# One head pair of a pooled attention taken from fp32 transposes on TensorE to fp16 parts and DMA transposes

## The chip, the core and the metric

The kernel runs on one core of a Trainium2 chip. The metric is the device time in microseconds of one execution. A core has five engines with their own in-order queues: TensorE (PE; its weight loads are listed as PEld), VectorE (DVE), ScalarE (ACT), GpSimd (POOL) and SyncE (SP), which here only issues DMAs to 16 DMA engines.

## The reference

Attention with pooled queries, then a feed-forward block (FFN), in fp32:

```python
q_pool = q.reshape(B, H, S // 2, 2, D).mean(axis=3)      # B=4, H=8, S=1152, D=64
scores = matmul(q_pool, k^T) / sqrt(D)
attn = softmax(scores)                                   # 576 x 1152 for each of 32 heads
x = matmul(attn, v), heads side by side                  # 2304 x 512
h = x @ w_in                                             # 512 -> 2048
g = relu(h) ** 2
out = g @ w_out                                          # 2048 -> 512
```

## The kernel before

**Pairs and chunks.** Two heads form a pair, so there are 16 pairs, four for each batch. A pair has nine chunks of 128 query rows, 144 chunks in all, numbered from 0. For a chunk the kernel computes on TensorE the scores against 1152 keys into PSUM (S, lines 739 to 760), on VectorE their maximum (MX, line 771), on ScalarE the exponential (EX, line 795), which leaves P as 128x1152 fp32 in SBUF. P must then be transposed, so that keys lie on partitions, before it is multiplied by V (PV). The transposed chunks lie in one tile, PT. A pair's chunks form two groups, r0 (four chunks) and r1 (five), and each group has one PV.

**Two ways to transpose.** For pairs listed in the option FV, P stays fp32: nine fp32 transposes on TensorE into PSUM (TP, line 836), copied to PT three at a time by ScalarE or VectorE (TC, lines 846 and 848), and a PV of 36 fp32 matmuls (line 947). For all other pairs P is split into two fp16 parts: the high part (HI, ScalarE, line 799), the rest (LO, GpSimd or VectorE, line 807); both are transposed by one DMA on SyncE's queue (TR, line 810), and the PV has three products, 108 fp16 matmuls (line 955). V is split in the same manner for these pairs (VA line 343 or 345, VD line 374), and a small addition (MB, lines 778 and 781) scales P. In the kernel before FV holds pairs 0 to 3, which are batch 0.

PT is shared by both ways, and they lay it out differently. Chunks of the other layout may be written only when every PV of the layout before has been computed; chunks of the same layout wait only for the PV whose columns they overwrite (function ringof). With the option PART the groups of pairs 2 and 3 come in the order r0 of pair 2, r0 of pair 3, r1 of pair 2, r1 of pair 3.

**FFN.** When a batch's pairs are done, blocks of 256 tokens go through the FFN: per block eight first products H (line 1119, 24 matmuls), each followed by a ReLU (HA, lines 1129 and 1131), a square in fp16 (G1, line 1134), a square in fp32 (G2, lines 1139 and 1142) and their difference (G3, line 1146), and eight second products O (line 1168, 12 matmuls). There are nine blocks. Their weights are split into fp16 parts at the start (lines 1222 to 1347). FFN work of earlier batches is mixed between the chunks of later ones; the last three blocks follow the last chunk.

**What sets the order.** The class Plan holds every step with its engine or engines, its cost and what it needs. It lists the steps by simulated start times; offsets by kind of step ('off', and 'off0' for the first part) and slacks by engine ('slPE' and so on) decide between ready steps, and which engine takes a step that has a choice. The program is then written out in that order, so every engine's queue is fixed. Seven buffers of 128x2304 fp16 hold P and its parts, two raw tiles hold loads, two PSUM tiles hold scores, and two PSUM banks hold everything else until the last chunk.

Of the kernel before, what the change touches and what calls it, by code (L numbers as in the profile page):

```python
# [16 lines left out]
AX = mybir.AxisListType  # L17
PSUM = bass.MemoryType.PSUM

CFG = {'SPLIT': 0, 'TURN': [], 'TURNB': [], 'WDP': ((1, 0), (1, 1), (1, 2), (1, 3)), 'WSP': 0.4394, 'WOF': 23.2581, 'MSP': 10.7319, 'pen': 4650.4498, 'bl': 16.0216, 'slPE': 66.7964, 'slACT': 353.0356, 'slDVE': 0.0, 'slPOOL': 569.0059, 'slSP': 247.8544, 'off': {'ED': 1246.3547, 'EX': 5849.5041, 'G1': -389.0426, 'G2': -104.1829, 'G3': 554.5948, 'GE': 1873.7106, 'GF': -32.4945, 'GM': -760.1485, 'GR': 210.7973, 'GS': 94.4545, 'H': 960.6071, 'HA': -234.5462, 'HI': -641.2151, 'KA': -143.9903, 'KC': -8.1783, 'KD': 872.723, 'KT': -553.181, 'KX': -147.2817, 'LF': 208.5276, 'LK': -464.9703, 'LO': 615.8798, 'LQ': 735.5594, 'LV': 186.7785, 'MB': 263.0646, 'MX': 219.6772, 'O': 959.2234, 'OD': -6.8812, 'PV': 582.1743, 'QA': -1778.9621, 'QC': -65.0614, 'QD': -30.2052, 'QK': 1295.5337, 'QQ': -170.0803, 'QS': 1636.5642, 'QT': 389.6557, 'QV': 96.5433, 'QX': 1378.7913, 'QY': 11.4121, 'RB': -182.8597, 'RT': -62.6818, 'RU': -185.4151, 'RV': 888.0764, 'S': 448.8179, 'ST': -370.0893, 'TC': -3741.4466, 'TP': 227.7703, 'TR': 3470.1614, 'U0': -286.6317, 'U1': -121.9166, 'U2': 428.2909, 'U4': -13.234, 'U5': -34.8662, 'UA': -25.2061, 'UB': 489.5818, 'UD': -136.1539, 'UG': -386.0049, 'UL': -18.9466, 'UM': 385.026, 'US1': 86.5628, 'US2': 126.1804, 'US3': 177.5466, 'VA': -449.2776, 'VD': -50.9897, 'W0': 92.9318, 'W1': -160.9693, 'W2': 2408.4173, 'W4': 41.9909, 'W5': -49.6702, 'WA': -177.1177, 'WD': 4887.2789, 'WG': 51.2485, 'WL': -84.1217, 'WM': -759.71, 'WS1': -97.3652, 'WS2': -484.1136, 'WS3': -24.1358, 'XA': 3.5042, 'XD': 344.6772, 'XM': 149.4019, 'XN': -648.326, 'XO': -302.7277, 'XQ': 72.8927, 'XR': 25.0451, 'XT': 74.8128, 'XU': -26.4071, 'XW': -53.316, 'aG1': 975.376, 'aG2': -8.3412, 'aG3': 1812.5384, 'aH': 945.5101, 'aHA': 95.0276, 'aO': 944.1552, 'aOD': 737.0717, 'aRB': -107.2593, 'aRT': -33.339, 'aRU': -29.5278, 'aRV': 101.1642, 'aST': -112.5231, 'aXA': -332.137, 'aXD': -1.658, 'aXM': -134.621, 'aXN': 37.6008, 'aXO': 26.3067, 'aXQ': 42.9163, 'aXR': 1688.4275, 'aXT': -68.0245, 'aXU': 17.1682, 'aXW': 186.1889, 'zG1': 91.0859, 'zG2': 58.4733, 'zG3': 647.1768, 'zH': -71.0289, 'zHA': -90.6818, 'zO': -226.9787, 'zOD': -96.8945, 'zRB': 31.1111, 'zRT': 315.2862, 'zRU': 90.4617, 'zRV': -0.3031, 'zST': -3.2166, 'zXA': -0.3901, 'zXD': -290.7, 'zXM': 77.2111, 'zXN': 89.9134, 'zXO': -46.2986, 'zXQ': 96.7, 'zXR': 171.8139, 'zXT': -141.9837, 'zXU': 189.9734, 'zXW': -22.7318}, 'off0': {'ED': -0.1938, 'EX': 44.7507, 'G1': 37.0992, 'G2': 58.5453, 'G3': -179.5235, 'GE': 422.2703, 'GF': -3.4782, 'GM': 45.9462, 'GR': -673.3064, 'GS': 105.2042, 'H': 24.4643, 'HA': -223.3679, 'HI': -0.3824, 'KA': -287.1981, 'KC': 265.8239, 'KD': 60.1455, 'KT': 47.8024, 'KX': -28.954, 'LF': 2579.7627, 'LK': 334.2631, 'LO': -615.0613, 'LQ': -324.4973, 'LV': -104.7173, 'MB': 34.3544, 'MX': -0.4589, 'O': 221.9113, 'OD': -64.4508, 'PV': -177.1018, 'QA': 354.2099, 'QC': 78.2737, 'QD': -44.0538, 'QK': -43.1499, 'QQ': 328.969, 'QS': 153.2762, 'QT': -555.006, 'QV': -66.5589, 'QX': -187.5264, 'QY': -268.1213, 'RB': -32.6021, 'RU': -78.4363, 'RV': 5.802, 'S': 2.838, 'ST': -2.5942, 'TC': 45.0906, 'TP': -907.5806, 'U0': 36.9458, 'U1': -33.4125, 'U2': 285.286, 'U4': 104.4439, 'U5': 15.7265, 'UA': 719.2255, 'UB': 70.692, 'UD': 144.5044, 'UG': 106.0304, 'UL': 11.0132, 'UM': 73.0092, 'US1': 161.6416, 'US2': -3.3033, 'US3': 328.9473, 'VA': 5.0083, 'VD': 0.3732, 'W0': 160.5816, 'W1': -301.2958, 'W2': -204.9077, 'W4': -25.4103, 'W5': -205.3827, 'WA': -279.8196, 'WD': -6.6893, 'WG': -22.2842, 'WL': -342.4531, 'WM': 192.4837, 'WS1': -321.4596, 'WS2': -444.2766, 'WS3': -35.6721, 'XA': 154.1639, 'XD': -16.0094, 'XM': 58.2004, 'XN': -133.1141, 'XO': 39.0783, 'XQ': -62.6032, 'XR': -9.301, 'XT': 225.4302, 'XU': -208.803, 'XW': -31.9494, 'aG1': -6.3492, 'aG2': -53.3067, 'aG3': -123.269, 'aH': -2.0139, 'aO': 367.1081, 'aOD': -23.0563, 'aRB': -38.5418, 'aRT': -62.2213, 'aRU': -52.5422, 'aRV': -10.1497, 'aST': -203.7505, 'aXD': -771.7661, 'aXM': -273.1333, 'aXN': -91.8521, 'aXO': 34.8573, 'aXQ': -0.2413, 'aXR': -502.6026, 'aXU': 52.3162, 'aXW': -13.8618, 'zG1': 8.5148, 'zG2': -475.2825, 'zG3': 47.993, 'zH': 315.6821, 'zHA': -17.051, 'zO': 53.7112, 'zOD': -299.6009, 'zRB': 117.4021, 'zRT': -17.2734, 'zRU': -54.008, 'zRV': 84.2467, 'zST': 346.2005, 'zXA': 239.278, 'zXD': -8.2809, 'zXM': -91.6437, 'zXN': -36.4568, 'zXO': 47.406, 'zXQ': -130.928, 'zXR': 322.459, 'zXT': -469.0206, 'zXU': -229.1112, 'zXW': -385.6444}, 'FV': (0, 1, 2, 3), 'PART': 1, 'QXD': (1, 2, 3, 4), 'MSC': (0, 1, 2, 3, 4, 5, 6, 7, 8, 9, 10, 11, 12, 13, 14, 15), 'FS': (0,), 'NSG': (12, 13, 14, 15)}  # L20
# [4 lines left out]

# [1433 lines left out]
```

## Time and profile before

| | us |
|---|---|
| three runs | 793.77, 796.21 (median), 802.07 |
| profiled execution | 796.25 |
| its span | 794.4 |
| PE busy | 743.8 (94%) |
| ACT busy | 589.7 (74%) |
| DVE busy | 571.4 (72%) |
| POOL busy | 350.1 (44%) |
| mean granted TensorE clock | 0.973 of 2.4 GHz |

The span runs from the first to the last instruction; 1.9 us of the profiled execution lie outside it. Busy shares are of the whole span; the kernel has a first part (weights, batch 0), a long middle part (chunks and FFN mixed) and a last part (FFN alone), so shares must be read by stretch.

### The profile page before, as it was taken

What the parts mean: (1) busy time and instruction counts of PE and PEld (TensorE: products, weight loads), DVE (VectorE), ACT (ScalarE), POOL (GpSimd) and SP (SyncE); (2) the same over time, 40 slices, a digit from 0 to 9 for tenths busy, and PEclk for the clock granted to TensorE, in tenths of its full rate; (3) what the DMA queues carried; (4) which work ended last, traced back from release to release, by engine and by line L of the source; (5) the groups of instructions that cost most, each with busy time, mean ns of one, the idle gap of its engine ahead of it and who ended that gap; (6) DMA issues with size and microseconds to landing.
All of it is one profiled execution on the core that took longest, in us unless ns stands there. A gap on an engine that the chain in (4) does not pass through costs nothing.

```text
span 794.4 us, 15338 instructions
## 1 busy us (share of the span) xinstructions
PE 743.8 (94%) x5998; PEld 491.7 (62%) x5998; DVE 571.4 (72%) x920; ACT 589.7 (74%) x874; POOL 350.1 (44%) x240
## 2 busy tenths in 40 slices
...
DMA  8686573417889999999999999999999991000011
GB/s 325 225 233 187 167 204 106 120 31 142 168 172 199 194 225 218 219 206 215 186 212 199 217 208 207 202 228 195 209 217 191 173 183 25 1 2 13 14 27 28
DMA packets 324840, 128.96 MB, mean 162 GB/s; under 512 B 307104, under 2 KB 307872, under 8 KB 324768
## 3 DMA queue, kind: packets, MB, share of 16 engines
...
## 4 chain that ended last, share of the span: by engine, by line
PE 78%; DVE 7%; ACT 5%; DMA 5%; issue 3%; SPq 1%; POOL 0%; DVEq 0%; ACTq 0%; POOLq 0%
PE ba L1168 17%; PE ba L1119 17%; PE s L760 12%; PE ba L955 10%; PE bt L1168 7%; PE bt L1119 6%; DVE s L771 3%; PE ba L836 3%; DMA region<-in_moe_w_in_dram 2%; PE ba L947 2%; ACT buf L795 2%; PE s L755 2%; DMA w<-in_moe_w_out_dram 2%; DVE PT L848 1%; ACT PT L846 1%
## 5 line engine op out<-in xcount | busy, mean ns | idle before, releaser
L771 DVE TENSOR_SCALAR_CACHE_REDUCE s<-s,esc 128x1152 f32<-128x1152 f32 x135 | 190.9, 1420 | 32.2 <-PE s L760 21.9
L1119 PEld LDWEIGHTS <-w 128*128 128x128 f16 x1728 | 169.4, 99 | 33.1 <-issue 7.0
L795 ACT ACTIVATE buf<-s,ca 128x1152 f32<-128x1152 f32 x144 | 174.4, 1212 | 14.2 <-DVE s L771 7.7
L807 POOL TENSOR_TENSOR buf<-buf,buf 128x1152 f16<-128x1152 f32 x53 | 130.9, 2472 | 54.1 <-ACT buf L799 44.2
L760 PE MATMUL s<-kT,qT 128*128 128x512 f16 x720 | 137.6, 330 | 9.3 <-ACT buf L795 9.0
L1168 PE MATMUL ba<-w,region 128*128 128x512 f16 x624 | 142.2, 379 | 1.3 <-ACT region L1129 0.7
L1168 PEld LDWEIGHTS <-region 128*128 128x128 f16 x864 | 82.8, 98 | 96.3 <-issue 2.5
L1119 PE MATMUL ba<-region,w 128*128 128x256 f16 x1104 | 128.7, 275 | 1.3 <-DVE x L1046 1.2
L799 ACT ACTIVATE buf<-buf 128x1152 f16<-128x1152 f32 x107 | 124.5, 1163 | 5.9 <-DMA PT<-buf 1.7
L760 PEld LDWEIGHTS <-qT 128*128 128x128 f16 x720 | 63.6, 100 | 66.9 <-issue 18.1
L807 DVE TENSOR_TENSOR buf<-buf,buf 128x1152 f16<-128x1152 f32 x55 | 77.1, 1404 | 14.4 <-ACT buf L799 14.1
L955 PE MATMUL ba<-PT,v 128*64 128x320 f16 (+1 forms) x1296 | 85.4, 290 | 0.0
L955 PEld LDWEIGHTS <-v 128*64 128x64 f16 x1296 | 70.8, 111 | 14.7 <-issue 7.1
L1146 POOL TENSOR_TENSOR region<-region 128x512 f16<-128x512 f32 x35 | 49.2, 1405 | 51.4 <-ACT region L1139 50.0
L1146 DVE TENSOR_TENSOR region<-region 128x512 f16<-128x512 f32 x37 | 29.1, 793 | 58.7 <-ACT region L1139 55.8
L836 PE MATMUL ba<-ident,buf 128*128 128x128 f32 x324 | 54.4, 296 | 14.8 <-ACT buf L795 5.5
L1134 ACT ACTIVATE region<-region 128x512 f16<-128x512 f32 x72 | 45.1, 626 | 20.3 <-PE bt L1168 17.3
L836 PEld LDWEIGHTS ba<-ident,buf 128*128 128x128 f32 x324 | 36.4, 148 | 30.7 <-ACT PT L846 8.7
L1168 PE MATMUL bt<-w,region 128*128 128x512 f16 x240 | 52.6, 379 | 0.0
L1142 POOL TENSOR_TENSOR region<-region 128x512 f32<-128x512 f32 x11 | 14.6, 1329 | 83.6 <-ACT region L1134 83.6
L846 ACT ACTIVATE PT<-ba 128x384 f32<-128x384 f32 x76 | 35.7, 490 | 18.6 <-PE ba L836 17.1
L1119 PE MATMUL bt<-region,w 128*128 128x256 f16 x432 | 48.7, 273 | 0.0
...
## 6 DMA issues: line engine op xcount, KB each, us to landing
...
```

What stands on the lines that cost most here:

```text
L760: nc.tensor.matmul(s[:, x, :w], lhsT=qt[:, l].rearrange("p c m -> p (c m)")[:, 128 * c0 + h : 128 * c0 + h + 255 : 2], rhs=rhs, **st)
L771: nc.vector.tensor_scalar(st3(), st3(), sc, 3e38, op0=ALU.mult, op1=ALU.min, accum_out=a[:, x : x + 1])
L795: nc.scalar.activation(P(), st3(), AF.Exp, bias=a[:, 1:2], scale=s1, accum_out=col)
L799: nc.scalar.activation(hl()[:, 0], P(), AF.Copy)
L807: e.tensor_tensor(out=hl()[:, 1], in0=P(), in1=hl()[:, 0], op=ALU.subtract)
L836: nc.tensor.matmul(t[:, y], lhsT=P()[:, c * 128 : (c + 1) * 128], rhs=ident, is_transpose=True, start=(y == 0), stop=(y == 2), skip_group_ ...
L846: nc.scalar.activation(out, t, AF.Copy)
L955: nc.tensor.matmul(px[h * 64 : (h + 1) * 64, 64 * r * (1 - h) : 64 * r * (1 - h) + N], lhsT=vv[:, h, kc, vl, :], rhs=p2(vi, r, h, 9 * pl + ...
L1119: nc.tensor.matmul(ph[:, f2], lhsT=w16[0][:, SLOT[f // 4], wl, a, f % 4 * 128 : (f % 4 + 1) * 128], rhs=xhl()[:, xl, a], start=(i == 0), s ...
L1134: nc.scalar.activation(gt[u][:, 0], rt[u % 2], AF.Square)
L1146: e.tensor_tensor(out=gt[u][:, 1], in0=rt[u % 2], in1=gt[u][:, 0], op=ALU.subtract)
L1168: nc.tensor.matmul(p[:, :DM], lhsT=g[:, gl, f % 2, tt * 128 : (tt + 1) * 128], rhs=w16[1][:, SLOT[f // 4], wl, f % 4], start=(f == 0 and g ...
```

## The change

FV loses pair 3, and the numbers that set the order are new (252 offsets and ten other numbers; the engines that may take a step are the same):

```diff
-CFG = {... 'WSP': 0.4394, 'WOF': 23.2581, 'MSP': 10.7319, 'pen': 4650.4498, 'bl': 16.0216, 'slPE': 66.7964, ...
+CFG = {... 'WSP': 1.0247, 'WOF': 22.4804, 'MSP': 10.4991, 'pen': 6462.0091, 'bl': 16.654, 'slPE': 128.9911, ...
...
-... 'FV': (0, 1, 2, 3), 'PART': 1, 'QXD': (1, 2, 3, 4), ...
+... 'FV': (0, 1, 2), 'PART': 1, 'QXD': (1, 2, 3, 4), ...
```

So the groups r0 of pair 2, r0 of pair 3, r1 of pair 2, r1 of pair 3 now change PT's layout three times instead of once after them.

SyncE's queue before, from pair 4's query transpose on (kT and qT are transposed keys and queries of a pair, PT<-buf is TR of a chunk): the first TR is pair 4's, behind the key and query transposes of pair 5.

```order
L646 DMA_TRANSPOSE qT_105<-half_100 128x9x128
L652 DMA qT_105<-qT_105 64x1152 x2
L633 DMA_TRANSPOSE kT_103<-buf_93 128x18x128
L455 DMA raw_102<-in_k_dram 128x2x576
L463 DMA raw_101<-in_q_dram 64x1152 x2
L455 DMA raw_101<-in_v_dram 128x2x576
L633 DMA_TRANSPOSE kT_104<-buf_98 128x18x128
L455 DMA raw_102<-in_k_dram 128x2x576
L646 DMA_TRANSPOSE qT_106<-half_100 128x9x128
L810 DMA_TRANSPOSE PT<-buf_95 128x18x128
L810 DMA_TRANSPOSE PT<-buf_93 128x18x128
```

And now: four TR of pair 3's r0 with a weight load and a load of values between them, then pair 4's keys and queries, then the TR of pair 3's r1.

```order
L810 DMA_TRANSPOSE PT<-buf_99 128x18x128
L1222 DMA w_1_91<-in_moe_w_out_dram 128x2x1024
L810 DMA_TRANSPOSE PT<-buf_98 128x18x128
L810 DMA_TRANSPOSE PT<-buf_94 128x18x128
L455 DMA raw_102<-in_v_dram 128x2x576
L810 DMA_TRANSPOSE PT<-buf_95 128x18x128
L646 DMA_TRANSPOSE qT_105<-half_100 128x9x128
L633 DMA_TRANSPOSE kT_103<-buf_97 128x18x128
L455 DMA raw_101<-in_k_dram 128x2x576
L652 DMA qT_105<-qT_105 64x1152 x2
L810 DMA_TRANSPOSE PT<-buf_97 128x18x128
L810 DMA_TRANSPOSE PT<-buf_93 128x18x128
```

Nine TR more stand ahead of pair 4's, and pair 5's keys and queries, which stood ahead of pair 4's first TR, now stand on either side of it.

ScalarE's queue before, in front of pair 4's first exponential, chunk 36 (the last row; sums_87 is the batch's row sums, L846 a copy of transposed P, L343 on w and v a high part of a weight or of V).

```order
L343 ACTIVATE v_0_107<-raw_101,psc 128x18x64
L1343 ACTIVATE w_1_91<-w_1_91,wS_1313 128x2048
L846 ACTIVATE PT<-ba_114 128x3x128
L846 ACTIVATE PT<-ba_115 128x3x128
L846 ACTIVATE PT<-ba_114 128x3x128
L846 ACTIVATE PT<-ba_115 128x3x128
L795 ACTIVATE buf_94,sums_86<-s_113,ca 128x1152
L846 ACTIVATE PT<-ba_115 128x3x128
L795 ACTIVATE buf_96,sums_87<-s_112,ca 128x1152
```

And now, in front of the same exponential (L1129, L1134 and L1139 are FFN steps, L778 is MB).

```order
L778 ACTIVATE ca<-ca,cols 128x1
L1134 ACTIVATE region<-region 128x512
L1139 ACTIVATE region<-region 128x512
L1129 ACTIVATE region<-ba_114 128x512
L1134 ACTIVATE region<-region 128x512
L1139 ACTIVATE region<-region 128x512
L778 ACTIVATE ca<-ca,cols 128x1
L1129 ACTIVATE region<-ba_115 128x512
L343 ACTIVATE half_100<-raw_102,psc 128x9x64
L1134 ACTIVATE region<-region 128x512
L1139 ACTIVATE region<-region 128x512
L795 ACTIVATE buf_94,sums_87<-s_112,ca 128x1152
```

The exponential of chunk 36 stood at place 162 of ScalarE's queue and stands at 184; FFN steps that came behind it come before it.

## Rows read from the trace of the kernel before

**Rows 1.** The page: busy time of each engine; share of the 16 DMA engines by 40 slices.
```profile
PE 743.8 (94%) x5998; PEld 491.7 (62%) x5998; DVE 571.4 (72%) x920; ACT 589.7 (74%) x874; POOL 350.1 (44%) x240
...
DMA  8686573417889999999999999999999991000011
```

**Rows 2.** Stretches: length; busy PE, PEld, DVE, ACT, POOL; clock; DMA share; GB/s.
```profile
160.00:200.00 40.00, 33.00 (x242) 20.55 (x243) 31.23 (x66) 38.03 (x53) 23.82 (x12) 0.98 0.47 93
200.00:229.00 29.00, 29.00 (x245) 21.27 (x244) 22.47 (x34) 23.75 (x36) 21.71 (x14) 0.91 0.82 150
229.00:300.00 71.00, 70.00 (x604) 46.58 (x602) 62.36 (x89) 61.06 (x92) 45.38 (x31) 1.00 1.11 211
...
600.00:652.00 52.00, 52.00 (x459) 34.11 (x458) 42.54 (x63) 44.08 (x64) 21.98 (x15) 1.00 1.00 179
652.00:794.00 142.00, 137.77 (x1006) 91.87 (x1004) 32.97 (x63) 46.58 (x74) 10.27 (x10) 0.99 0.09 20
```

**Rows 3.** The chain of waits between 229 and 652 us, shares by line.
```profile
by line: PE ba L1168 27.8%; PE ba L1119 23.8%; PE s L760 19.9%; PE ba L955 17.3%; PE s L755 2.3%; issue 1.5%; DMA raw<-in_v_dram 1.1%; DVE s L771 0.9%; ACT buf L795 0.8%; DVE region L1046 0.7%; DVE buf L807 0.6%; PE ba L591 0.5%; POOL half 
```

**Rows 4.** Groups by line (the first of all shapes): count | busy, mean ns | idle before.
```profile
L760 PE MATMUL s<-kT,qT 128*128 128x512 f16 x720 | 137.6, 330 | 9.3 <-ACT buf L795 9.0
L836 PE MATMUL ba<-ident,buf 128*128 128x128 f32 x324 | 54.4, 296 | 14.8 <-ACT buf L795 5.5 <-DVE PT L848 4.6 <-ACT PT L846 3.4
L947 PE MATMUL ba<-PT,v 128*64 128x320 f32 x144 | 20.3, 435 | 0.6 <-DVE PT L848 0.6
L947 PE MATMUL ba<-PT,v 128*64 128x256 f32 x144 | 16.4, 382 | 0.3 <-ACT PT L846 0.3
L955 PE MATMUL ba<-PT,v 128*64 128x320 f16 x648 | 47.7, 306 | 0.0
L955 PE MATMUL ba<-PT,v 128*64 128x256 f16 x648 | 37.7, 273 | 0.0
```

**Rows 5.** The same view: work of ScalarE, and the two forms of LO.
```profile
L846 ACT ACTIVATE PT<-ba 128x384 f32<-128x384 f32 x76 | 35.7, 490 | 18.6 <-PE ba L836 17.1 <-DVE PT L848 0.2
L1134 ACT ACTIVATE region<-region 128x512 f16<-128x512 f32 x72 | 45.1, 626 | 20.3 <-PE bt L1168 17.3 <-DVE region L1131 1.6
L1139 ACT ACTIVATE region<-region 128x512 f32<-128x512 f32 x59 | 37.2, 630 | 1.8
L778 ACT ACTIVATE ca<-ca,cols 128x1 f32<-128x1 f32 x42 | 12.3, 292 | 21.4 <-DVE s L771 20.3 <-DVE xs L363 0.3
L343 ACT ACTIVATE buf<-raw,psc 128x1152 f16<-128x1152 f32 x4 | 5.0, 1242 | 0.0
L799 ACT ACTIVATE buf<-buf 128x1152 f16<-128x1152 f32 x107 | 124.5, 1163 | 5.9 <-DMA PT<-buf 1.7
L807 POOL TENSOR_TENSOR buf<-buf,buf 128x1152 f16<-128x1152 f32 x53 | 130.9, 2472 | 54.1 <-ACT buf L799 44.2 <-issue 7.7 <-POOL esc L368 1.1
L807 DVE TENSOR_TENSOR buf<-buf,buf 128x1152 f16<-128x1152 f32 x55 | 77.1, 1404 | 14.4 <-ACT buf L799 14.1
```

**Rows 6.** The source view of line 810: durations, first and last start; time to landing.
```profile
L810 SPq DMA_TRANSPOSE PT<-buf x108: 2400/2840/5931, 191.1 to 652.0; - x108
...
DMA to landing us min/median/max: 4.5/5.2/8.4
```

**Rows 7.** SyncE's timeline: start, duration, instruction, count.
```profile
258.81 1.40 SPq L463 DMA_DIRECT2D raw<-in_q_dram  x2
260.31 10.09 SPq L810 DMA_TRANSPOSE PT<-buf  x3
...
280.09 4.28 SPq L810 DMA_TRANSPOSE PT<-buf  x1
```

**Rows 8.** ScalarE's timeline: the exponential of chunk 56.
```profile
266.79 1.22 ACT L795 ACTIVATE buf<-s,ca 128x1152 f32<-128x1152 f32 x1
```

**Rows 9.** TensorE's timeline: the first FFN products, in brackets the idle time ahead.
```profile
182.09 2.78 PE L1119 MATMUL ba<-buf,w 128*128 128x256 f16 x24 [0.18 <-DVE psc L601]
199.31 5.28 PE L1119 MATMUL ba<-buf,w 128*128 128x256 f16 x24 [3.68 <-DVE region L1046]
```

2 lines of the change are left out of this document (1 added, 1 removed).

## The prediction

> **What bounds the kernel now.** I read the page first [rows 1]. TensorE is busy 94% of the span, and the DMA slices stand at 9 from about 220 us on, until they drop to 0 and 1 near 655 us. So two resources are nearly full over most of the span, and which one sets the pace has to be read by stretch. The windows [rows 2] show three parts. Up to about 229 us neither is full: between 160 and 200 us TensorE works 33.00 of 40 us and the DMA share is 0.47, while ScalarE works 38.03 of 40. From 229 to 652 us TensorE is full (70.00 of 71, 52.00 of 52) and the DMA share is 1.11 at the front and 1.00 at the back. From 652 us on only FFN is left: TensorE 137.77 of 142 us, DMA 0.09.
>
> The chain of waits over the middle [rows 3] is nearly all TensorE: products of the FFN, of the scores and PV, and 1.1% DMA. Read alone it says that TensorE is the bound. But the source view of the transposes [rows 6] and SyncE's timeline [rows 7] say something else. 108 TR start between 191.1 and 652.0 us, one in 4.3 us, and in the timeline one instruction starts as the one before it ends (258.81 + 1.40 to 260.31), so at that place the queue has no gap. Chunk 56 shows what it means: its exponential starts at 266.79 us and takes 1.22 [rows 8], HI takes 1.16 and LO on GpSimd 2.47 [rows 5], so P could go out at 271.6. Its TR starts at 280.09 [rows 7]: it stands 8.5 us behind the queue. The middle is therefore held from both sides: the queue sets when P arrives, and TensorE fills what is left with FFN work. Saving TensorE time there shortens the run only as far as the stream of TR moves too.
>
> **The change, part by part.**
>
> *TensorE.* Removed are 9 x 9 = 81 fp32 transposes of 54.4 / 324 = 0.168 us, 13.6 us, and two fp32 PV of (20.3 + 16.4) / 8 = 4.6 us each, 9.2 us. Added are two fp16 PV of (47.7 + 37.7) / 24 = 3.6 us, 7.1 us [rows 4]. The sum is -15.7 us; the small products by which pair 3's values get their scale take some of it back, so I use -15. This work lies ahead of pair 4, where TensorE is not full: at the share of 160 to 200 us, 33.00 / 40 = 0.83 [rows 2], some 12 us of it are on a path.
>
> *The DMA queue.* Nine more TR of 2.84 us, 25.6 us [rows 6]. They go out ahead of pair 4's first TR (191.1), among slices of DMA that read 3, 4, 1 and 7 tenths [rows 1], so I cost their bandwidth at nothing. The cover is the 0.53 of the share that is free between 160 and 200 us, 21 us, and more ahead of it; were it gone, 25.6 us would come upon every later TR. Bounds: 0 and +25.6; I take 0, for the rows at the place itself are the nearest.
>
> The Trainium skill, page "VectorE: DVE Perf Modes", sections "The three transpose paths" and "Rules for kernel authors", speaks against the change: it gives 390 ns for a 128x128 bf16 block on TensorE and 1309 ns by DMA, and advises TensorE where PSUM can take the result. By it the 9 x 18 blocks would be an estimated 212 us of the queue. The trace does not agree on the figure: 18 blocks go out in 2.84 us [rows 6], 0.16 us each, no more than an fp32 block on TensorE.
>
> *ScalarE.* 17 copies of transposed P go (-8.3 us at 0.490), nine HI come (+10.5 at 1.163) [rows 5]; the total is nearly unchanged, but its place is not. By the two lists of ScalarE's order, ahead of chunk 56's exponential there are now nine more HI (+10.5), seven more G1 and G2 each (+8.8 at 0.626 and 0.630), five more fp16 splits of V (+6.2 at 1.242), seven more MB (+2.0 at 0.292), and the 17 copies less (-8.3) [rows 5]: +19.2 us. The exponential comes later by what ScalarE cannot fit into its idle time. It worked 38.03 + 23.75 + 61.06 = 122.8 of the 140 us from 160 to 300 us, 0.88; if it fills up to the 0.95 of 160 to 200 us [rows 2], the 107 us up to this exponential give 0.07 x 107 = 7.5 us. Left are 11.7 us, and the 8.5 us in which this chunk's P waited for the queue hide most of that. So the stream of TR from there on is **3 us late**. Bounds: 0 (ScalarE fills up completely) and +11 (it fills up by nothing: 19.2 - 8.5). I take 3, from the row of the same stretch.
>
> *VectorE and GpSimd.* There are ten fewer copies on VectorE. Of the 117 LO, GpSimd now has 76 where it had 53, VectorE 41 where it had 55 [rows 5]. GpSimd gains 23 x 2.47 = 57 us of LO and has 350.1 us of work in all [rows 1]; it stays far from full. VectorE gets 20 us free. For a chunk with no time in the queue a LO on GpSimd is 1.07 us later than one on VectorE; where P waits 8.5 us that is hidden. I cost it at nothing and keep it as a rival.
>
> *Layouts of PT.* Three switches in place of one. At each of the two new ones towards DMA the TR must wait for the PV before. I cost them at nothing in the forecast, because first FFN products exist by 182.09 us [rows 9] and can stand in for pair 3's second wait; the first wait is a rival.
>
> *What comes back later.* From pair 6's products on, TensorE has 15 us less to do than before at the same place of the stream. It can gain them only if TR follow. At 600 to 652 us the share is 1.00 and at 229 to 300 us 1.11 [rows 2], so the later queue has room, but the bound from below is 0 and from above 15 (TensorE's own saving). The rows say that both are full and not which gives way first, so I take half, -7. The part after the last PV, 142 us [rows 2], is the same work in both and stays.
>
> **Sum.** +3 - 7 = -4 us. The profiled execution took 796.25 us (span 794.4), 0.04 above the median of 796.21, so the sum needs no shift: 796.25 - 4 = **792 us**.
>
> **The rivals.**
>
> *A, the forecast:* the queue takes back most of TensorE's gain. 792 us; by its bounds (+11 with nothing back is 807, 0 with all 15 back is 781) and half of each, its own range is 787 to 800. Chance 0.48, of which 0.06 lie below 788.2.
>
> *B, TensorE is the bound all along.* For it: the chain [rows 3] with 1.1% DMA, and 52.00 of 52 us. Against it: the wait of chunk 56's P for its TR [rows 7, 8]. Then the 12 us that are on a path reach the end: 796 - 12 = 784 us. Chance 0.26.
>
> *C, slower: the new switch of layout at pair 3's r0.* Its four TR may not go before pair 2's r0 has its PV, and pair 3's r0 product needs all four: 4 x 2.84 + 5.2 us to landing [rows 6] = 16.6 us. In that time TensorE has no FFN work (the first H stands after it) and pair 2's r1 may not be transposed into PT, since it has the other layout. Two score tiles let it compute the scores of two chunks, 2 x 137.6 / 144 = 1.9 us [rows 4]. It idles some 14 us, and may then run at half clock: 24 matmuls took 5.28 us after 3.68 us of idle time, against 2.78 [rows 9]. It decides once the wait goes beyond the 1.9 us, and if the later part gives nothing back: 796 + 14 = 810 us. Against it: TensorE has 17% idle time there already, part of which may be the same wait. Chance 0.18. Only by such a wait, not by its price for a block, would the advice of the Trainium skill hold.
>
> *D, LO on GpSimd.* Where P does not wait for the queue, 23 LO that come 1.07 us later hold the stream up; a third of them in such places are 8 x 1.07 = 9 us on top of the forecast: 801 us. For it: 1.00 of DMA at the end, where the queue has room and P is late. Against it: VectorE is less loaded, so LO can start sooner. Chance 0.08.
>
> **How the numbers follow.** The likeliest is A, 792 us. About 1% is what a measurement of this kernel can tell from no change: 788.2 and 804.2 us. Faster: B's 0.26 and 0.06 of A, 0.32. Slower: C's 0.18, 0.02 of A, and 0.02 of D, 0.22. The same: 0.46. The range reaches from B's side, some 2 us below its 784, to C's 810: 782 to 810.
>
> **What would show it.** TensorE's busy time falls to about 729 us and the last stretch after the last TR stays at 142 us: then the sum on TensorE is right, and the run's change is the move of the last TR away from 652.0. For A, chunk 56's exponential starts later than 266.79 by about 12 us, its TR by some 3, and the last TR starts 4 us earlier. For B, the exponential and the stream start earlier and DMA shares in the middle rise. For C, an idle stretch of some 14 us on TensorE stands ahead of pair 3's first fp16 product with DMA as the releaser, and slow matmuls after it. For D, the chain of waits shows LO of GpSimd in the middle. The forecast is wrong if the middle's queue packs tighter than 1.11, or if ScalarE fills its idle time so fully that chunk 56 is not late.

## The result, and the profile after

The changed kernel takes 806.9 us (median of four runs, 803.8 to 808.7) against 797.0 before: 1.1% slower, ratio 1.0113 with a 95% interval of 1.0075 to 1.0151. Forecast were 792 us and a range of 782 to 810; the time lies in the range, but the kernel became slower where a gain was forecast; the chance given to slower was 0.22.

The page, as [rows 1]: busy times, and the DMA share by slices of a fortieth of the span.

```profile
PE 736.9 (92%) x5964; PEld 487.3 (61%) x5964; DVE 580.1 (72%) x922; ACT 595.3 (74%) x876; POOL 376.7 (47%) x247
...
DMA  8687548738999999999999999999999992000011
```

TensorE works 6.9 us less, the span (804.9 us) is 10.5 longer, so TensorE idles 17.4 us more. The groups of TensorE, as [rows 4] (the fp16 PV of one group is 54 matmuls; 108 are the two groups of a pair):

```profile
L760 PE MATMUL s<-kT,qT 128*128 128x512 f16 x720 | 141.2, 337 | 13.0 <-ACT buf L795 13.0
...
L836 PE MATMUL ba<-ident,buf 128*128 128x128 f32 x243 | 39.2, 288 | 12.0 <-ACT PT L846 6.8 <-DVE PT L848 3.3 <-ACT buf L795 1.8
...
L947 PE MATMUL ba<-PT,v 128*64 128x320 f32 x108 | 15.2, 435 | 0.0
L947 PE MATMUL ba<-PT,v 128*64 128x256 f32 x108 | 14.0, 420 | 2.1 <-DVE psc L601 1.9 <-ACT PT L846 0.3
...
L955 PE MATMUL ba<-PT,v 128*64 128x320 f16 x702 | 51.1, 300 | 0.8 <-DMA PT<-buf 0.7
L955 PE MATMUL ba<-PT,v 128*64 128x256 f16 x702 | 43.2, 280 | 2.5 <-DVE psc L601 1.6 <-DMA PT<-buf 0.4 <-DVE region L1131 0.4
```

Transposes 54.4 to 39.2, fp32 PV 36.7 to 29.2, fp16 PV 85.4 to 94.3: -13.8 us, close to the -15 of the sum. Some of it goes at once: the scores of line 760 take 141.2 us where they took 137.6, the same matmuls, with a lower granted clock in the stretches from 300 to 400 us below.

The windows show where the rest went (columns as in [rows 2]); first the changed kernel from 120 us on, then three stretches of the kernel before that [rows 2] lack.

```profile
120.00:160.00 40.00, 27.22 (x256) 17.85 (x255) 35.16 (x62) 26.75 (x40) 17.51 (x11) 0.91 0.79 186
160.00:200.00 40.00, 34.62 (x279) 25.46 (x278) 32.17 (x51) 38.57 (x51) 26.92 (x14) 1.00 0.54 96
229.00:300.00 71.00, 70.74 (x570) 46.12 (x569) 61.06 (x87) 61.34 (x91) 43.68 (x28) 1.00 1.08 207
300.00:340.00 40.00, 31.97 (x229) 17.60 (x228) 31.13 (x53) 31.73 (x49) 23.77 (x12) 0.84 1.07 210
340.00:400.00 60.00, 51.49 (x449) 37.34 (x447) 48.09 (x86) 46.65 (x71) 33.82 (x21) 0.82 1.07 198
663.00:805.00 142.00, 137.21 (x1004) 91.69 (x1003) 34.43 (x64) 44.70 (x72) 9.58 (x11) 1.00 0.09 20
```

```profile
120.00:160.00 40.00, 33.43 (x282) 21.46 (x280) 31.51 (x63) 31.66 (x49) 9.90 (x7) 1.00 0.38 106
300.00:340.00 40.00, 40.00 (x306) 22.52 (x306) 29.54 (x47) 29.98 (x44) 20.49 (x15) 1.00 1.11 209
340.00:400.00 60.00, 53.10 (x467) 37.04 (x463) 49.74 (x90) 52.96 (x78) 34.10 (x24) 0.89 1.06 205
```

Two holes: 120 to 160 us (27.2 of 40 us, clock 0.91) and 300 to 400 us (83.5 of 100, clock 0.82 to 0.84; before 93.1). The last stretch is the same 142 us.

The first hole lies among the switches of PT's layout. TensorE's timeline has pair 3's first fp16 product (54 matmuls of line 955) and pair 2's r1 product (line 947); SyncE's has the last transfer ahead of pair 3's r1 and the first of its TR; SyncE's list of waits, 100 to 230 us, says what held TR (total, times, longest).

```profile
149.18 3.14 PE L955 MATMUL ba<-PT,v 128*64 128x256 f16 x54 [1.62 <-DVE psc L601]
...
169.88 5.07 PE L947 MATMUL ba<-PT,v 128*64 128x320 f32 x36
```

```profile
150.42 1.15 SPq L652 DMA_DIRECT2D qT<-qT  x2
175.03 9.14 SPq L810 DMA_TRANSPOSE PT<-buf  x3
```

```profile
SPq L810 <- DVE PT L848: 14.4, 1, 14.4
SPq L810 <- PE ba L947: 9.5, 2, 9.0
```

From 151.6 to 175.0 us SyncE stands with pair 3's r1 TR at the head of its queue: pair 2's r1 may go into PT only after the fp16 product of 149.18, needs its transposes and copies, and gives PT free when its own product ends at 175.0. That is a wait of the queue. TensorE's own waits from 120 to 160 us name exponentials (6.6 us), a scale (1.6) and loads (2.3), and no TR, so it is not shown that the switch makes the hole.

In the second hole TensorE has no FFN left. Its timeline: scores at full rate, the last product of batch 0's FFN, scores that wait for exponentials, the first H of batch 1.

```profile
312.77 1.14 PE L760 MATMUL s<-kT,qT 128*128 128x512 f16 x6
313.74 2.75 PE L1168 MATMUL ba<-w,region 128*128 128x512 f16 x12
...
335.11 2.08 PE L760 MATMUL s<-kT,qT 128*128 128x512 f16 x6 [1.91 <-ACT buf L795]
...
363.34 2.78 PE L1119 MATMUL ba<-region,w 128*128 128x256 f16 x24
...
369.88 2.13 PE L755 MATMUL s<-kT,qT 128*64 128x512 f16 x12 [3.42 <-ACT buf L795]
```

Six score products of line 760 take 2.08 us there and 1.14 us at 312.77; the granted clock is 0.84 from 300 to 340 us and 1.00 before. So there is no FFN product from 316.5 to 363.3 us, 46.9 us. In the kernel before that gap is 23.9 us long; its timeline has the last product of batch 0's FFN and the first H of batch 1 at

```profile
332.76 2.75 PE L1168 MATMUL ba<-w,region 128*128 128x512 f16 x12
...
359.38 2.78 PE L1119 MATMUL ba<-region,w 128*128 128x256 f16 x24
```

The stream of transposes, as [rows 6], and chunk 56, as [rows 7, 8]: its exponential (ScalarE) and its TR (SyncE).

```profile
L810 SPq DMA_TRANSPOSE PT<-buf x117: 2397/2862/6071, 127.7 to 663.3; - x117
```

```profile
280.07 1.20 ACT L795 ACTIVATE buf<-s,ca 128x1152 f32<-128x1152 f32 x1
```

```profile
291.37 4.10 SPq L810 DMA_TRANSPOSE PT<-buf  x1
```

The exponential is 13.3 us late (12 were forecast), its TR 11.3 (3 were forecast), and the last TR 11.3 (4 us early was forecast). Chunk 56 has 15 H and 9 O ahead of its exponential, 8 and 8 in the kernel before, so part of its delay is FFN work done earlier.

Much below is read from ScalarE's timelines, at the exponentials of chunks 36, 72 and 143, of one profiled execution each (that of e9 was its slowest, 795.2 us):

| us | start of chunk 36 | 36 to 72 | 72 to 143 |
|---|---|---|---|
| before | 176.0 | 169.0 | 301.9 |
| changed | 196.9 (+20.9) | 150.4 (-18.6) | 310.0 (+8.1) |
| e1 TR halved, before | 175.6 | 168.5 | 300.5 |
| e2 TR halved, changed | 196.9 | 150.1 | 306.5 |
| e5 first part cut | 179.0 | 166.3 | 302.5 |
| e6 middle cut | 178.0 | 168.5 | 300.7 |
| e9 middle and TR cut | 180.8 | 162.2 | 302.9 |
| e10 list of before from 72 | 200.0 | 152.8 | 303.9 |
| e11 list of change from 72 | 178.9 | 169.3 | 311.9 |
| e12 list of before from 36 | 187.7 | 171.3 | 303.3 |

Chunk 36 scatters by some 5 us between runs that have the same list up to there (175.6 to 180.8); the other two columns scatter less. In the changed kernel eight H stand ahead of chunk 40's scores, in the kernel before two: FFN work went from the second column into the first, and the two nearly cancel. At chunk 72 both have batch 0's FFN done (16 H, 16 O), and the changed kernel is 2.3 us late, although TensorE had 14 us less to do. Another 8 us go after it by this table; but the border is not clean, since some steps of batch 1 stand ahead of chunk 72's exponential in one list and behind it in the other (shown with e10).

### The profile page after: what moved, and what is told of

Its sections match the earlier page's. It is cut to its first block, busy times and chain, and to the rows that moved or that the text cites. A ratio compares the mean times of both kernels' runs of the same rounds, so it can differ in the third digit from the quotient of the medians.

```text
span 804.9 us, 15284 instructions
## 1 busy us (share of the span) xinstructions
PE 736.9 (92%) x5964; PEld 487.3 (61%) x5964; DVE 580.1 (72%) x922; ACT 595.3 (74%) x876; POOL 376.7 (47%) x247
## 4 chain that ended last, share of the span: by engine, by line
PE 62%; DMA 10%; DVE 9%; ACT 8%; issue 5%; POOL 4%; SPq 1%; DVEq 0%; ACTq 0%; POOLq 0%
PE ba L1119 14%; PE ba L1168 13%; PE s L760 9%; PE ba L955 9%; PE bt L1168 6%; PE bt L1119 6%; DMA PT<-buf 4%; DVE s L771 2%; POOL buf L807 2%; ACT buf L795 2%; DMA region<-in_moe_w_in_dram 2%; PE ba L947 2%; DMA raw<-in_v_dram 1%; DMA w<-in_moe_w_out_dram 1%; PE s L739 1%
## 5 line engine op out<-in xcount | busy, mean ns | idle before, releaser
L807 POOL TENSOR_TENSOR buf<-buf,buf 128x1152 f16<-128x1152 f32 x76 | 187.5, 2470 | 103.1 <-ACT buf L799 91.0
L760 PE MATMUL s<-kT,qT 128*128 128x512 f16 x720 | 141.2, 337 | 13.0 <-ACT buf L795 13.0
L799 ACT ACTIVATE buf<-buf 128x1152 f16<-128x1152 f32 x115 | 133.8, 1163 | 6.5 <-DMA PT<-buf 0.8
L1146 POOL TENSOR_TENSOR region<-region 128x512 f16<-128x512 f32 x39 | 54.3, 1394 | 105.8 <-ACT region L1139 105.7
L955 PE MATMUL ba<-PT,v 128*64 128x256 f16 (+1 forms) x1404 | 94.3, 290 | 3.2 <-DVE psc L601 1.6
L955 PEld LDWEIGHTS <-v 128*64 128x64 f16 x1404 | 79.1, 111 | 18.5 <-issue 9.1
L807 DVE TENSOR_TENSOR buf<-buf,buf 128x1152 f16<-128x1152 f32 x41 | 63.0, 1536 | 15.9 <-ACT buf L799 13.4
L1134 ACT ACTIVATE region<-region 128x512 f16<-128x512 f32 x72 | 44.9, 623 | 23.4 <-PE bt L1168 19.1
L1146 DVE TENSOR_TENSOR region<-region 128x512 f16<-128x512 f32 x33 | 28.7, 871 | 30.9 <-ACT region L1139 29.2
L836 PE MATMUL ba<-ident,buf 128*128 128x128 f32 x243 | 39.2, 288 | 12.0 <-ACT PT L846 6.8
L374 DVE SCALAR_TENSOR_TENSOR buf<-raw,psc,buf 128x576 f16<-128x576 f32 x31 | 44.9, 1451 | 0.3 <-POOL buf L345 0.3
L1139 ACT ACTIVATE region<-region 128x512 f32<-128x512 f32 x67 | 42.2, 629 | 2.0
L836 PEld LDWEIGHTS ba<-ident,buf 128*128 128x128 f32 x243 | 25.7, 142 | 25.0 <-ACT PT L846 11.7
```

The costliest lines, as they stand in the source:

```text
L374: nc.vector.scalar_tensor_tensor(out=o, in0=x, scalar=s, in1=h, op0=ALU.mult, op1=ALU.subtract)
L760: nc.tensor.matmul(s[:, x, :w], lhsT=qt[:, l].rearrange("p c m -> p (c m)")[:, 128 * c0 + h : 128 * c0 + h + 255 : 2], rhs=rhs, **st)
L799: nc.scalar.activation(hl()[:, 0], P(), AF.Copy)
L807: e.tensor_tensor(out=hl()[:, 1], in0=P(), in1=hl()[:, 0], op=ALU.subtract)
L836: nc.tensor.matmul(t[:, y], lhsT=P()[:, c * 128 : (c + 1) * 128], rhs=ident, is_transpose=True, start=(y == 0), stop=(y == 2), skip_group_ ...
L955: nc.tensor.matmul(px[h * 64 : (h + 1) * 64, 64 * r * (1 - h) : 64 * r * (1 - h) + N], lhsT=vv[:, h, kc, vl, :], rhs=p2(vi, r, h, 9 * pl + ...
```

## The experiments

**Is the queue the bound, and who takes TensorE's saving?** Both kernels with half of every TR, in their own order:

```diff
-nc.sync.dma_start_transpose(out=pslot(vi, j, False), in_=hl().rearrange("p l k -> p (l k)"))
+nc.sync.dma_start_transpose(out=pslot(vi, j, False)[:, 0:9], in_=hl()[:, 0])
...
-rhs=p2(vi, r, h, 9 * pl + kc, False)
+rhs=p2(vi, r, h, kc, False)
```

> The kernel before with the same order on every engine, but each TR sends only the nine blocks of the high part, and the PV reads the high part where it read the low part, so that it has the same 108 matmuls (its result lacks the low part). Theory Q (the transposes' queue sets the pace of the middle): the last TR, at 652.0 us before, comes at least 10 us earlier, and the time falls to 786 or below. Rival P (TensorE sets the pace, the queue is only full): the time stays within 4 us of 797.

> The changed kernel with the same edit: TR of nine blocks, order and matmuls as they are. Theory Q (the queue takes the 15 us that TensorE saves): with the queue no longer full the saving shows, and this kernel ends 8 to 18 us ahead of e1_half_before, below 780 us. Rival W (late exponentials or a wait at the switch of PT's layout cost the time, whatever the queue does): it ends later than e1_half_before, as the changed kernel does against the kernel before (about +10 us).

e1: 797.1 us, ratio 1.0001 (0.9967 to 1.0034). e2: 803.0 us, 1.0056 (1.0026 to 1.0085), 5.9 us behind e1 and not ahead of it, as rival W has it. The halved TR leave the changed kernel's chunk 36 where it was (196.9), so the length of the TR is not what makes it late. About half of the loss goes with them (1.0056 against 1.0113, intervals that just overlap), by the table behind chunk 72 (306.5 against 310.0). The middle of e1, and its TR:

```profile
229.00:300.00 71.00, 70.34 (x605) 46.60 (x602) 61.24 (x88) 61.22 (x91) 46.44 (x31) 1.00 0.70 141
```

```profile
L810 SPq DMA_TRANSPOSE PT<-buf x108: 1243/1322/4486, 190.7 to 647.1; - x108
```

The share fell from 1.11 to 0.70, and nothing came of it in the kernel before. The queue alone does not set the pace: theory Q falls. The Trainium skill, page "Perfetto Trace Analysis", section "What 'DMA-bound' means", calls a kernel bound on the DMA sequencer when its track is solid DMA slices; [rows 7] show such a track, and e1 that the kernel was not bound by it alone.

**Is it TensorE?** The kernel before, in its own order, with TensorE's work cut for pair 3, and for pairs 4 to 6:

```diff
+ny = 1 if n == 3 else 3      # e5: TP
+nk = 1 if n == 3 else NC     # e5: PV
...
+ps = ps[:NC] if n in (4, 5, 6) else ps      # e6: PV
```

> The kernel before in its own order; for pair 3 alone TensorE does less: one of three transposes of each TP, and PV over one of nine key blocks (54 transposes and 64 fp32 matmuls fewer, 17.3 us of TensorE by the rows of before; pair 3's result is wrong). Nothing is added. Theory F (TensorE does not set the pace of the first part, so what is saved there is lost): 793 to 798 us, at most 4 us gained. Rival B (TensorE is the bound all along): at least 12 us gained, 785 or below.

> The kernel before in its own order; the PV of pairs 4, 5 and 6 compute one of their three products (216 matmuls fewer, 14.2 us of TensorE, from some 200 to 330 us; the result lacks two products there). Theory F with the hole (batch 0's FFN is over before batch 1's values are ready, so what TensorE saves there only opens the hole at 345 us further): 792 to 798 us. Rival M (the same saving is worth its full size where TensorE is full): 782 to 786 us.

e5: 800.2 us, 1.0037 (1.0011 to 1.0063). e6: 799.4 us, 1.0026 (0.9995 to 1.0057). 17.3 and 14.2 us of TensorE were to go by the rows; by the pages its busy time is 11.3 and 13.1 us less (732.5 and 730.7 against 743.8), and nothing is gained. In e6's middle TensorE has room, and the queue is as full as before:

```profile
229.00:300.00 71.00, 63.84 (x462) 40.19 (x460) 60.34 (x87) 59.66 (x89) 44.28 (x30) 0.98 1.12 210
```

That kills rival B for the kernel before, in the first part and in the middle. e9 makes both cuts of the middle at once, those of e1 and e6:

> The kernel before in its own order with both cuts at once: TR of nine blocks as in e1_half_before and one product of three in the PV of pairs 4, 5 and 6 as in e6_cut_middle. Each alone gave nothing. Theory C (TensorE and the transposes' queue bind together, each covers the other): 783 to 789 us, since both give way. Rival D (a third thing, the way of a chunk through scores, maximum, exponential and the split, sets the pace of chunks 36 to 72): 793 to 799 us.

789.8 us, 0.9899 (0.9825 to 0.9972). Chunks 36 to 72 take 162.2 us where each cut alone left 168.5. So TensorE and the queue bind together there, as theory C has it, though the time lies just outside its 783 to 789. Some 6 to 8 us come back of the 13 that TensorE saves (by the interval 2 to 14); what keeps the rest is not shown.

**Is it the place of the FFN?** e7 ties H and O of batch 0 to the chunks where the kernel before has them, by one more need for each step in the plan; e8 puts back the offsets of the first block (22 kinds of step, not the 17 of its text).

```diff
-add(("H", j, u), {"PE": 2640}, [("XD", j)] + ...      # e7, O likewise
+add(("H", j, u), {"PE": 2640}, [("XD", j)] + ([("S", both(int([38 + 1.2 * u, 57 + u][m]))[0])] if m < 2 else []) + ...
...
-'aH': 793.638, 'aO': 1061.6044, ...      # e8
+'aH': 945.5101, 'aO': 944.1552, ...
```

> The changed kernel with its numbers, but H and O of batch 0's two blocks must wait in the plan for the scores of the chunks beside which they stand in the kernel before (H from chunk 38, O from 46; second block from 57 and 63). Theory F: the hole of 316 to 363 us in the changed kernel comes from FFN work that was used up too early; with it spread again the hole shrinks to 15 us or less and the time falls to 797 or below. Rival: the hole is only moved, because the chunks' own production (ScalarE, VectorE, GpSimd) sets the pace; 802 to 812 us.

> The changed kernel, but the offsets of batch 0's first FFN block alone (the 17 whose key begins with a) are those of the kernel before; in the order H begins at chunk 38 as there. Theory F: at or below 797 us, as e7_paced. Rival: 802 us or more.

810.7 us, 1.0194 (1.0151 to 1.0238), and 824.9 us, 1.0352 (1.0305 to 1.0398). Holding FFN work back does shrink the second hole in e7, and opens another in the first part:

```profile
160.00:200.00 40.00, 26.61 (x142) 14.01 (x142) 29.66 (x46) 35.69 (x43) 23.99 (x10) 0.79 0.52 93
300.00:340.00 40.00, 37.91 (x309) 23.99 (x307) 30.47 (x49) 32.93 (x50) 22.77 (x15) 1.00 1.04 191
```

TensorE works 37.91 us where the changed kernel has 31.97, and 26.61 where that has 34.62; chunk 72 comes at 354.5 us, 7 us later. So the hole is only moved, as the rival has it; that the chunks' production is the reason is not shown. e8 has no H ahead of chunk 36 either and reaches chunk 72 at 347.1 us, as early as the changed kernel; it loses its time later.

**The form of pair 3 or the order?** Each alone, first with the list found by the rules:

```diff
-'FV': (0, 1, 2)      # e3: the new numbers
+'FV': (0, 1, 2, 3)
...
-'FV': (0, 1, 2, 3)   # e4: the old numbers
+'FV': (0, 1, 2)
```

> The kernel before (pairs 0 to 3 in fp32) with the new numbers for the order. If the new order by itself is the cost, the time is about 807 us or more, since TensorE's 15 us are not saved either. If pair 3's parts and DMA transposes are the cost, it is within 5 us of 797.

> Pair 3 in fp16 parts with the old numbers for the order. If pair 3's form is the cost: 805 us or more, with the first TR of pair 4 10 us later than 191.1, as in the changed kernel (201.9). If the order is the cost: 790 to 799 us.

828.3 us, 1.0403 (1.0347 to 1.0458), and 825.4 us, 1.0366 (1.0310 to 1.0422). Numbers found for one form give a poor list for the other, so these two can't divide the 10 us. e10 to e12 therefore write the steps out from a fixed list, made of a piece of each kernel's own list (the steps done ahead of an exponential in one list's order, all others in the other's; each step keeps the engine that its list gives it). In words, not in the kernels' code:

```diff
-seq = plan.order(("EX", NSTEP - 1))
+seq = changed[ahead of EX 72] + before[rest]      # e10, pair 3 in fp16
+seq = before[ahead of EX 72] + changed[rest]      # e11, pair 3 in fp32
+seq = changed[what before has ahead of EX 36] + before[rest]      # e12, pair 3 in fp16
```

> Pair 3 in fp16 parts. All steps that the changed kernel does ahead of chunk 72's exponential stand in its order, all later ones in the order of the kernel before. From chunk 72 on both kernels have the same steps left, yet the changed kernel loses 8 us there (2.3 us late at chunk 72, 10.3 at chunk 142). Theory O (the order found anew costs these 8 us): 795 to 801 us. Rival (what pair 3's form left behind costs them): 804 us or more.

> The opposite of e10: pair 3 in fp32 and the order of the kernel before up to chunk 72, the order of the changed kernel from there. Theory O: 801 to 807 us. Rival: 794 to 799 us.

> Pair 3 in fp16 parts and in the changed kernel's order, but only for the steps that the kernel before has done ahead of chunk 36's exponential; all else, batch 0's FFN too, stands where the kernel before has it. It is pair 3's new form by itself. Theory F (TensorE's saving falls where it does not set the pace): 794 to 801 us. Rival C of the prediction (the switch of layout costs): 804 us or more. Rival B (TensorE is the bound): 787 us or less.

e10: 805.9 us, 1.0104 (1.0026 to 1.0183). e11: 809.1 us, 1.0120 (1.0048 to 1.0192). e12: 814.4 us, 1.0183 (1.0067 to 1.0298). By the whole times e10 says the rival: with the old list from chunk 72 on it is only 1 us faster than the changed kernel. e11 says that the new list costs, more than theory O asked for. The table's last column seems to decide it: with the old list from chunk 72 on it is 300.5 to 303.9 us, with the new one 310.0 and 311.9 (306.5 with TR halved). But e10's gain there, 6.1 us, depends on where the border is set. ScalarE's timeline of e10, then of the changed kernel, have one step of batch 1 (line 1058) and chunk 72's exponential in opposite order:

```profile
351.92 1.04 ACT L1058 ACTIVATE buf<-region 128x1024 bf16<-128x1024 f32 x1
352.87 1.20 ACT L795 ACTIVATE buf<-s,ca 128x1152 f32<-128x1152 f32 x1
```

```profile
347.27 1.20 ACT L795 ACTIVATE buf<-s,ca 128x1152 f32<-128x1152 f32 x1
...
351.79 1.04 ACT L1058 ACTIVATE buf<-region 128x1024 bf16<-128x1024 f32 x1
```

Counted from chunk 71's exponential, e10 takes 315.0 us and the changed kernel 317.8 (the kernel before 307.2, e11 318.3, e12 308.7); counted from the first H of batch 1 to chunk 143 they take 287.8 and 294.0. So e11 shows that the new list costs time behind chunk 72 in the kernel before, and it stays open how much of the changed kernel's 8 us it is. e12 has pair 3's form, the new list up to chunk 36 and everything else, batch 0's FFN too, in its old place: 14 us late at chunk 72, and TensorE stands in the first part:

```profile
160.00:200.00 40.00, 25.58 (x124) 13.71 (x125) 28.31 (x50) 29.85 (x35) 17.32 (x10) 0.70 0.48 96
```

**The switches or the fp16 way itself?** PART 0 takes pair 2's groups first, then pair 3's, so that the layout changes once:

```diff
-'PART': 1
+'PART': 0      # e13: changed kernel; e14: e4; e15: kernel before
...
-'FV': (0, 1, 2)
+'FV': (0, 1)   # e16
```

> The changed kernel and its numbers with PART 0: r0 and r1 of pair 2 come first, then those of pair 3, so that PT's layout changes once. Theory S (the switches cost the first part: SyncE stood 23 us, from 151.6 to 175.0, before pair 3's r1 could go out): no TR waits more than 8 us, and chunk 36's exponential starts before 190 us (196.9 in the changed kernel, 176.0 before) with FFN no further ahead than its order says. The whole time can move by some 25 us for the order alone (e3, e4), so the first part is what tells: if it is as late as in the changed kernel or TensorE has as little to do there, S falls.

> As e13, with the old numbers for the order: e4_pair3_only with one switch in place of three. Theory S: at least 8 us faster than e4 (825.4) with chunk 36 at least 8 us earlier than there (211.9). Rival (the switches are hidden; the new form costs by its ScalarE work): within 5 us of e4.

> A control: the kernel before, pair 3 in fp32, with PART 0. There is one switch in either case. If PART 0 is worth something by itself, this run is faster than 797 us and e14's gain is not the switches'. Theory S: not faster than the kernel before.

> The changed kernel and its numbers with pair 2 in fp16 parts too (FV 0, 1), so that the four groups of pairs 2 and 3 have one layout and PT changes once. TensorE has some 15 us less to do than in the changed kernel, ScalarE and the queue more. Theory S: chunk 36 comes earlier than in the changed kernel (196.9) although two pairs take the longer way, and no TR waits 20 us. Rival (the fp16 way itself costs the first part time): chunk 36 later than 200 us.

| | us | ratio | switches | FFN products ahead of chunk 36 | chunk 36 at us |
|---|---|---|---|---|---|
| e4 | 825.4 | 1.0366 | 3 | 7 H, 1 O | 211.9 |
| e14 | 819.2 | 1.0304 (1.0261 to 1.0346) | 1 | none | 186.3 |
| e15 | 805.3 | 1.0124 (1.0088 to 1.0161) | 1, pair 3 in fp32 | none | 177.5 |
| e13 | 830.2 | 1.0424 (1.0381 to 1.0466) | 1 | none | 191.7 |
| e16 | 845.4 | 1.0629 (1.0577 to 1.0681) | 1 | 4 H | 227.5 |

SyncE's waits for a TR up to 225 us, the largest of e4 (for pair 2's product) and the largest of e14:

```profile
SPq L810 <- PE ba L947: 32.9, 2, 24.7
```

```profile
SPq L810 <- PE ba L955: 6.7, 1, 6.7
```

With the old numbers, chunk 36 comes 25.6 us earlier with one switch than with three, but most of that is FFN work: e4's TensorE does seven H and an O ahead of it, some 22 us at 2.78 and 2.75 us each, and e14's none. TensorE's timeline of e4 has four of them at

```profile
189.87 2.78 PE L1119 MATMUL ba<-buf,w 128*128 128x256 f16 x24
193.47 8.02 PE L1119 MATMUL ba<-buf,w 128*128 128x256 f16 x72
```

A fairer comparison is between kernels with pair 3 in fp16 and no FFN ahead of chunk 36, though their lists differ in other steps too. With three switches it comes at 186.0 (e8), 187.7 (e12) and 193.0 us (e7), with one at 186.3 (e14) and 191.7 (e13); with pair 3 in fp32 at 175.6 to 180.8. So the new form makes the first part some 5 to 17 us later, and the number of switches does not show there, though the one long wait for PT is gone with them: the longest of a TR are 4.7 (e13), 6.7 (e14) and 7.1 us (e16) against 14.4 and 9.0 in the changed kernel. So nothing here bears out theory S as the cause of the late chunk 36. The 6.2 us between e4 and e14 stand between what S (8) and its rival (5) asked for, and within what lists made by the rules differ by (PART 0 alone makes e15 8 us slower than the kernel before, and e13 23 us slower than the changed one). With one switch in both and the old numbers, pair 3's form costs 13.9 us over all (e14 against e15), about what e12 has with three (15.7 over the kernel before of its session). What in the form costs it, ScalarE's steps, the loads behind the TR or another thing, is not shown.

## Why the prediction was wrong

- **TensorE's sum** was right: -15 forecast, -13.8 measured, and 17.4 us of idle time took its place. Rival B (12 us on a path) is refuted for the kernel before by e5 and e6.
- **"What comes back later"** is one step that failed: -7 was taken, half of the bounds, and nothing came back; the stream is as late at its end (11.3 us) as at chunk 56, and between them 6 to 12 us. Both resources were full, and I took half of TensorE's gain for what two full resources leave. e1, e6 and e9 show what they do leave: none for one, some 8 us only for both.
- **"3 us late"** is the other, and as large: chunk 56's TR is 11.3 us late. ScalarE's part of the term was right in size: 18.1 more us of its work ahead of the exponential (19.2 were forecast), which is 13.3 us late (12). But the 8.5 us in which P waited for the queue did not hide the rest. The queue ahead of this TR has no gap from 261.2 us on, and P still waits: the whole stream had come late, its pair 4 by 10.8 us.
- So the two terms were +11.3 and 0 in place of +3 and -7, which is the 10 us at the end. Why the stream is late stays open. **"Layouts of PT"** at nothing is not refuted: the switches hold SyncE for 23 us, and without them chunk 36 is no earlier. **Rival C** came near in time (810) by luck: its sign is not there, as TensorE waits 1.6 us ahead of pair 3's first product, for VectorE.
- **The new list** had no term. By the table it costs 8.1 us behind chunk 72, between chunks 72 and 92 (95.1 us against 86.4); e11 bears this out and e10 does not.
- **Nine more TR at nothing** stands as far as their bandwidth goes (share 0.54 from 160 to 200 us, and e2).
- **Rival D** was not tried by itself and is not refuted. VectorE was to get 20 us free and is busier by 8.7 us (LO 14.1 less; 13 more ReLU 8.9, the low parts of line 374 11.4 more). D's sign stands in the changed kernel's chain from 229 to 663 us, LO of GpSimd with 3.8%, beside landings of TR, where [rows 3] have LO of VectorE with 0.6%; the lists of e10 to e12 carry the choice of engine too:

```profile
by line: PE ba L1168 20.2%; PE ba L1119 19.8%; PE s L760 14.1%; PE ba L955 14.1%; DMA PT<-buf 7.6%; issue 5.0%; POOL buf L807 3.8%; PE s L755 1.7%; DMA qT<-half 1.6%; DVE s L771 1.4%; DMA raw<-in_v_dram 1.4%; ACT buf L799 1.3%; SPq L810 0.8
```

- A slip without effect: the DMA slices stand at 9 from 238 us on, not from 220.

In one line: TensorE's saving was worth nothing because TensorE did not hold the pace alone, and the stream of TR came 11 us late and stayed so; pair 3's form makes the first part late whatever the number of switches, and how the list shares in the 10 us is open.

The Trainium skill's advice to transpose on TensorE (page "VectorE: DVE Perf Modes", section "Rules for kernel authors") is in line with the result, since taking pair 3 off TensorE gained nothing (ratio 1.0113), though not by the time of a block: 18 blocks took 2.86 us in the queue.
